# Attention with the weighted sum in full float32 on two halves of the array's columns

## The chip, the cores and the metric

One core of one Trainium2 chip runs the whole program. The metric is device time in microseconds (us), the median of three runs. A core has a matrix engine (TensorE, PE in the rows; its loads of the stationary operand are listed as PEld), VectorE (DVE), ScalarE (ACT), GpSimd (POOL) and the queues that issue DMAs (SP and ACT here). The engines run at the same time and wait for one another through semaphores; each works through its own list of instructions in order.

## The reference

The program chains three blocks. Attention is masked by a hash: a query sees only keys with the same six sign bits. Then comes a gated block with a mix over positions, and a residual block.

```python
mask = q_bucket[:, :, :, None] == k_bucket[:, :, None, :]
scores = scale * np.matmul(q, k.transpose(0, 1, 3, 2))
scores = np.where(mask, scores, -1000000000.0)
attn = np.exp(scores - np.max(scores, axis=-1, keepdims=True))
attn = attn / (np.sum(attn, axis=-1, keepdims=True) + 1e-09)
out = np.matmul(attn, v)                      # (2, 8, 768, 64)
# gated block, x is (2, 768, 512)
h = np.maximum(x @ w_in, 0.0)                 # 512 -> 1024, halves u and v
v_n = (v - mu) / np.sqrt(var + 1e-06)
v_s = np.einsum('ts,bsd->btd', w_spatial, v_n) + b_spatial[None, :, None]
x = (u * v_s) @ w_out                         # 512 -> 512
# residual block
ch = np.maximum(layernorm(x) * g_ln @ w_ch1, 0.0) @ w_ch2   # 512 -> 2048 -> 512
return x + ch
```

All matrices are float32, the weights `w_in`, `w_out`, `w_ch1` and `w_ch2` arrive as 64-bit floats. There are 2 batches, 8 heads, 768 positions and a head width of 64.

## The kernel before

**Tiles.** A tile is 128 queries of one head: 6 per head, 96 in all, in the list `order` (batch, head, group, tile). Two tiles make a group (`GRP = 2`), so there are 48 groups. `attn_step(i)` writes the work of step i: the transposes of tile i, the scores of tile i+2, the row maximum and the exponentials of tile i+1, and the weighted sum of the group that ended at tile i-1.

**Two kinds of product.** Where a float32 product is wanted exactly, the kernel mostly splits both operands into a high part of the type float32r and a rest, and adds the three products high-high, high-rest, rest-high (`mm3`). A product of plain float32 operands, as in `mismatch` (L245, output `pm`), is one call, and stands in the trace as two records.

**One tile.** `scores` (L303, `sc`) multiplies queries by 768 keys. `masked_max` (L314, DVE) takes the row maximum out of PSUM into `x`, `exps` (L327, ACT) the exponentials. `transposes` (L343, `pt`) turns the tile's six blocks of 128 x 128 around, three to a PSUM bank. ACT copies each bank out as float32r, `eh` (L352). For the first bank DVE takes the rest, `el` (`e_lo`, L360). For the second bank of every tile of batch 0, and of every other tile of batch 1 (`ES`), ACT copies to `es` (L347), and GpSimd makes `eh` (L77) and `el` (L86). `head_prep3` loads a head's values `vv` and GpSimd splits them as well (`vs`).

**Weighted sum.** `weighted` (L372, `po`) issues twelve matmuls for a group: six key tiles with `eh`, six with `el`. Each has the two parts of the values side by side as its 128 columns and 256 queries moving. The two halves of the result are then added: ACT copies the lower partitions' partner out as `ol` (L376), DVE adds (L378). `normalized` divides by the sums after every second head (`zr`, `zw`, `pz`, L383 to L393).

**Conversions.** The 64-bit weights of the gated block are converted in twelve pieces during attention, at the steps `CONV_AT`: ACT issues the load and takes the magnitude (L102), DVE makes five passes (L103 to L107), GpSimd adds (L111), ACT and GpSimd split (L80, L86). The result stays in SBUF for batch 0, in pieces of 1 MB of a ring of five (`WB`), and is written to DRAM, from where `reload` fetches it for batch 1.

**Stages.** From step 60 (`M0`) the gated block of batch 0 (`moe1(0)`) is woven into the steps of batch 1's attention: projections `pv`, mix `pg`, transposes `ptr`, output `py`. After the last step comes `moe1(1)`, with the first five pieces of the residual block, then the rest of that block (`up`, `pc`; `down`, `acc`) with 32 more conversions. The order on each engine is set by the tile scheduler, which lists the instructions by a timeline of its own; `issue_after` pins keep some of them behind others.

## Time and profile before

| | us |
|---|---|
| three runs: median (lowest, highest) | 748.74 (748.3, 752.26) |
| the profiled execution | 745.25 |
| its span | 743.5 |
| PE busy in it | 688.4 (93%) |
| DVE busy | 468.0 (63%) |
| ACT busy | 339.1 (46%) |
| POOL busy | 333.9 (45%) |

The busy shares are means over unlike stages, so the rows further down cut the span at four points: the first exponentials' maximum (13.4), the first projection of the gated block (186.2), the end of batch 0's gated block (356.5), and 480. A PE record lasts until its result is written, and the next one starts before that; the time that a run of matmuls takes is read from start to start.

### The profile page before, as it was taken

The numbers are of one execution on the slowest core, as the hardware profiler recorded it, in microseconds if no ns is written. First come the engines' busy times: TensorE is split into PE (matmuls) and PEld (weight loads), VectorE is DVE, ScalarE is ACT, GpSimd is POOL, SyncE is SP. The second block draws the span as 40 slices with busy tenths as digits, with TensorE's granted clock in tenths as the row PEclk, the third lists the DMA queues.
The fourth block names the chain that finished last, engine by engine and source line by source line (L and its number), as shares of the span: only waits on it lengthen the run. The fifth ranks groups of instructions, "written<-read, shape, count | busy, mean of one in ns | idle before, by whom it ended". The sixth has DMA issues, their size and how long they took to land.

```text
span 743.5 us, 10402 instructions
## 1 busy us (share of the span) xinstructions
PE 688.4 (93%) x3580; PEld 567.5 (76%) x3580; DVE 468.0 (63%) x873; ACT 339.1 (46%) x679; POOL 333.9 (45%) x358
## 2 busy tenths in 40 slices
PE   7899988899899998999889999799988999999996
PEld 6688867688788877888677887678766788888885
DVE  4677989889786964545399648776998712112112
ACT  3687867787566655545346332443323300100100
POOL 2788898998586672421035233235444400000000
PEclk9999999999999999999998999989999999999999
DMA  5645655657526336243703433343233101001001
GB/s 143 158 123 150 168 167 153 179 150 212 173 65 173 92 82 163 66 133 143 276 29 142 121 123 132 131 153 114 85 106 93 57 1 56 1 0 57 1 0 58
DMA packets 52519, 82.31 MB, mean 111 GB/s; under 512 B 7050, under 2 KB 36286, under 8 KB 50930
## 3 DMA queue, kind: packets, MB, share of 16 engines
q1 hardware_dynamic: 29714, 47.56, 22.8%
q10 hardware_dynamic: 22752, 34.08, 14.4%
q8 instruction: 29, 0.48, 0.3%
q14 instruction: 24, 0.20, 0.1%
HBM read 49.03 MB, written 12.58 MB: 83 GB/s over the span
## 4 chain that ended last, share of the span: by engine, by line
PE 49%; DVE 16%; DMA 11%; POOL 11%; issue 6%; ACT 5%; SPq 1%; ACTq 0%; DVEq 0%; POOLq 0%
PE acc L751 12%; PE pc L453 11%; PE pv L453 6%; DMA f_w<-in_w 5%; PE sc L303 4%; PE pg L453 4%; PE po L372 4%; PE pt L343 3%; POOL el L86 3%; PE py L453 2%; DMA wst_sp<-in_w_spT 2%; DVE f_w L105 2%; POOL f64c_w L111 2%; DVE f64c_w L107 2%; POOL eh L77 1%
## 5 line engine op out<-in xcount | busy, mean ns | idle before, releaser
L751 PE MATMUL acc<-w2t,ch 128*128 128x512 f32 x576 | 145.3, 397 | 6.9 <-DVE ch L742 6.1
L453 PE MATMUL pc<-xh,w1t 128*128 128x512 f32 x576 | 146.1, 400 | 3.4 <-DVE xh L735 3.2
L751 PEld LDWEIGHTS acc<-w2t,ch 128*128 128x128 f32 x576 | 107.4, 189 | 34.8 <-DVE ch L742 9.4
L453 PEld LDWEIGHTS pc<-xh,w1t 128*128 128x128 f32 x576 | 109.8, 191 | 30.2 <-ACT f64c_w L102 3.2
L742 DVE SCALAR_TENSOR_TENSOR ch<-pc,ch 128x512 fp32r<-128x512 f32 x48 | 32.9, 686 | 112.2 <-ACT ch L741 112.2
L327 ACT ACTIVATE x<-x,nb 128x768 f32<-128x768 f32 x96 | 89.5, 933 | 29.4 <-DVE x L314 29.3
L314 DVE TENSOR_SCALAR_CACHE_REDUCE x<-sc 128x768 f32<-128x768 f32 x96 | 89.6, 948 | 19.0 <-PE sc L303 11.3
L303 PE MATMUL sc<-ks,qs 128*128 128x512 f32 (+3 forms) x384 | 83.8, 353 | 8.0 <-issue 4.5
L343 PE MATMUL pt<-ident,x 128*128 128x128 f32 x576 | 84.1, 275 | 5.0 <-ACT es L347 2.8
L741 ACT ACTIVATE ch<-pc 128x512 fp32r<-128x512 f32 x48 | 28.4, 592 | 125.4 <-PE pc L453 124.7
L111 POOL TENSOR_TENSOR f64c_w<-f_w,f64c_w 128x512 f32<-128x512 f32 x32 | 44.7, 1400 | 89.6 <-DVE f64c_w L107 76.0
L343 PEld LDWEIGHTS pt<-ident,x 128*128 128x128 f32 x576 | 68.1, 141 | 15.6 <-ACT es L347 4.0
L86 POOL TENSOR_TENSOR el<-es,eh 128x384 fp32r<-128x384 f32 x72 | 78.3, 1089 | 3.0
L453 PE MATMUL pv<-w_in,act_x 128*128 128x512 f32 x288 | 75.6, 418 | 4.1 <-DMA w_in<-ws_in 3.5
L360 DVE TENSOR_TENSOR el<-pt,eh 128x384 fp32r<-128x384 f32 x120 | 64.0, 548 | 22.6 <-ACT eh L352 18.1
L453 PEld LDWEIGHTS pv<-w_in,act_x 128*128 128x128 f32 x288 | 56.6, 201 | 17.3 <-DMA w_in<-ws_in 4.0
L303 PEld LDWEIGHTS sc<-ks,qs 128*128 128x128 f32 (+1 forms) x384 | 57.3, 192 | 15.3 <-issue 5.6
L352 ACT ACTIVATE eh<-pt 128x384 fp32r<-128x384 f32 x120 | 56.1, 487 | 27.7 <-PE pt L343 26.3
L372 PE MATMUL po<-eh,vs 128*128 128x256 f32 x288 | 52.0, 304 | 7.1 <-POOL eh L77 4.9
L77 POOL TENSOR_SCALAR eh<-es 128x384 fp32r<-128x384 f32 x72 | 41.5, 579 | 36.9 <-ACT es L347 36.9
L372 PE MATMUL po<-el,vs 128*128 128x256 f32 x288 | 49.7, 290 | 1.2 <-DVE el L360 0.4
L372 PEld LDWEIGHTS po<-eh,vs 128*128 128x128 f32 x288 | 39.7, 190 | 13.2 <-POOL eh L77 7.3
(127 smaller groups left out, 981.7 us busy)
## 6 DMA issues: line engine op xcount, KB each, us to landing
f_w<-in_w ACTq DMA_DIRECT2D x32, 512.0 KB
ks<-k SPq DMA_DIRECT2D x48, 192.0 KB
qs<-q SPq DMA_DIRECT2D x144, 64.0 KB
wst_sp<-in_w_spT ACTq DMA_DIRECT2D x12, 384.0 KB
f_in<-in_w_in ACTq DMA_DIRECT2D x8, 512.0 KB
ws_in<-w_in ACTq DMA_DIRECT2D x4, 1024.0 KB
w_in<-ws_in SPq DMA_DIRECT2D x4, 1024.0 KB
vv<-in_v SPq DMA_DIRECT2D x16, 192.0 KB
```

Source lines behind the costliest of these rows:

```text
L77: nc.gpsimd.tensor_scalar(dst, src, 1.0, 0.0, op0=ALU.mult, op1=ALU.add)
L86: nc.gpsimd.tensor_tensor(dst, src, hi.bitcast(F32), op=ALU.subtract)
L111: nc.gpsimd.tensor_tensor(cf, tf, cf, op=ALU.add)
L303: nc.tensor.matmul(sc[:, csl], qs[:rows, i, qsl], ks[:rows, i, csl], start=(i == 0), stop=(i == 1))
L314: last["max"] = nc.vector.tensor_scalar(x, t["sc"], MASKED, FMAX, op0=ALU.min, op1=ALU.min, accum_out=nb,).ins
L327: last["exp"] = nc.scalar.activation(t["x"], t["x"], AF.Exp, bias=t["nb"], scale=-1.0, accum_out=z_sum[b][:, n, h : h + 1]).ins
L343: nc.tensor.transpose(pt[:, i, :], t["x"][:, kt * P : (kt + 1) * P], ident)
L352: nc.scalar.activation(eh, pt, AF.Copy)
L360: nc.vector.tensor_tensor(gr["el"][:, sl, qsl], t["pt"][c], gr["eh"][:, sl, qsl].bitcast(F32), op=ALU.subtract)
L372: nc.tensor.matmul(po[:, :GW], w, gr[e][:, kt, :], start=(n == 0), stop=(n == len(parts) - 1))
L453: mm = nc.tensor.matmul(ps, lh(i), rh(j), start=(n == 0), stop=(n == tot - 1)).ins
L751: last["mm"] = nc.tensor.matmul(accs[c][t], ch[:, i, t * P : (t + 1) * P], w2t[f][:, j, 0, :], start=(start and n == 0), stop=(stop and n ...
```

## The change

The exponentials are no longer split. A group's tile is one float32 tile `e`; ACT copies the first bank of each tile into it, DVE the second (plain copies out of PSUM, L340 and L342 in the new numbering). The values stay float32 as loaded. The weighted sum is six float32 matmuls with 64 columns each; the even key tiles write partitions 0 to 63 of the bank, the odd ones partitions 64 to 127, through the lower and the upper half of the array's columns. The two halves are added as before. It is issued one step later (`PO = 2`), the sums of a pair of heads another step, and the division two steps after that. `e` has three buffers.

The conversions start at step 5 instead of 20 and end at 57, and come in the order `w_out`, v half of `w_in`, u half. All three are kept in DRAM, in blocks of 2 MB. Two slots of 2 MB hold the v half, the u half, `w_out` and then the v and u halves and `w_out` of batch 1, each fetched when a slot is free. `w_out`, converted first, stays in the tile `vn` only until it is written out. The pieces of `w_spatial` are loaded from SP instead of ACT, have a tile for each part, and the mix uses the rests first.

```diff
-    CONV_AT = (20, 26, 32, 38, 43, 48, 52, 56, 62, 67, 72, 77)
+    CONV_AT = (5, 9, 14, 19, 24, 29, 34, 39, 44, 49, 53, 57)
-    AT = (-9, -8, -7, -4, 0)
-    ES = ((1,), (1, 0))
-    WB = 5
+    AT = (-10, -7, -6, -4, 0)
+    PO = 2
+    EB = 3
...
-            nc.scalar.dma_start(out=st, in_=src)
+            nc.sync.dma_start(out=st, in_=src)
...
-        vs = ap.tile([P, NKT, 2, D], F32R, tag="vs", name=f"vs_{nm}")
-        split_hi(vs[:, :, 0, :], vv)
-        split_lo(vs[:, :, 1, :], vv, vs[:, :, 0, :])
-        heads[b, h]["vs"] = vs
+        heads[b, h]["vv"] = vv
...
+            gr["e"] = ap.tile([P, NKT, GW], F32, tag="e", name=f"e_{b}_{h}_{g}", bufs=EB)
...
-            eh = gr["eh"][:, c * 3 : c * 3 + 3, qsl]
-            if c == 1 and ES[b][(g * GRP + j) % len(ES[b])]:
-                es = ap.tile([P, 3, P], F32, tag="es", name=f"es_{jm}", bufs=2)
-                nc.scalar.activation(es, pt, AF.Copy)
-                split_hi(eh, es)
-                split_lo(gr["el"][:, c * 3 : c * 3 + 3, qsl], es, eh)
+            e = gr["e"][:, c * 3 : c * 3 + 3, qsl]
+            if c == 0:
+                nc.scalar.activation(e, pt, AF.Copy)
             else:
-                nc.scalar.activation(eh, pt, AF.Copy)
+                nc.vector.tensor_copy(e, pt)
...
-        for n, (kt, e) in enumerate(parts):
-            w = vs[:, kt].rearrange("p a d -> p (a d)")
-            nc.tensor.matmul(po[:, :GW], w, gr[e][:, kt, :], start=(n == 0), stop=(n == len(parts) - 1))
+        for kt in range(NKT):
+            a = kt % 2 * D
+            nc.tensor.matmul(
+                po[a : a + D, :GW], heads[b, h]["vv"][:, kt], gr["e"][:, kt], start=(kt < 2), stop=(kt >= NKT - 2)
+            )
...
-        if 0 <= i - 1 < NT and order[i - 1][3] == GRP - 1:
-            weighted(*order[i - 1][:3])
+        if 0 <= i - PO < NT and order[i - PO][3] == GRP - 1:
+            weighted(*order[i - PO][:3])
+        for late, e in ((1, summed), (3, normalized)):
...
+        for key, src, at in (("out", w_out, 0), ("v", w_in, HF), ("u", w_in, 0)):
...
+    def moe_tile(key, b):
+        wp[key, b] = mp.tile([P, 2, KFT, HF], F32R, tag="w", name=f"w_{key}_{b}", bufs=2)
+        return wp[key, b]
...
+            if t == NQT - 1:
+                reload("out", b)
...
+        if b == 0:
+            reload("v", 1)
...
-    reload(w_in_pieces() + w_out_pieces(), 1)
+    reload("u", 1)
```

The matrix engine, around the weighted sum of group 1 of head 3 (`po_3_1`), batch 0, before. `sc` are scores, `pt` transposes; the last number counts equal instructions in a row.

```order
L303 MATMUL sc_4_0_0_1050<-ks_4_0_996,qs_4_0_991 128x512 x2
L343 MATMUL pt_3_2_0_0_1037<-ident,x_3_2_0_1025 128x128 x3
L343 MATMUL pt_3_2_0_1_1042<-ident,x_3_2_0_1025 128x128 x3
L372 MATMUL po_3_1_1060<-eh_3_1_950,vs_3_791 128x256 x6
L343 MATMUL pt_3_2_1_0_1081<-ident,x_3_2_1_1055 128x128 x3
L372 MATMUL po_3_1_1060<-el_3_1_951,vs_3_791 128x256 x3
L343 MATMUL pt_3_2_1_1_1086<-ident,x_3_2_1_1055 128x128 x3
L372 MATMUL po_3_1_1060<-el_3_1_951,vs_3_791 128x256 x3
```

The same place on the same engine after:

```order
L299 MATMUL sc_4_0_0_909<-ks_4_0_863,qs_4_0_858 128x512 x2
L337 MATMUL pt_3_2_0_0_899<-ident,x_3_2_0_882 128x128 x3
L337 MATMUL pt_3_2_0_1_904<-ident,x_3_2_0_882 128x128 x3
L337 MATMUL pt_3_2_1_0_928<-ident,x_3_2_1_914 128x128 x3
L337 MATMUL pt_3_2_1_1_933<-ident,x_3_2_1_914 128x128 x3
L351 MATMUL po_3_1_946<-e_3_1_838,vv_3_690 64x256 x6
```

Twelve matmuls in three runs, between transposes, have become six in one run behind all the transposes of the group that follows.

GpSimd in the steps of heads 3 and 4, batch 0, before (`eh`, `el` and `vs` are the split parts, `f64c` a conversion):

```order
L77 TENSOR_SCALAR eh_3_1_950<-es_3_1_0_961 128x3x128
L86 TENSOR_TENSOR el_3_1_951<-es_3_1_0_961,eh_3_1_950 128x3x128
L77 TENSOR_SCALAR eh_3_1_950<-es_3_1_1_1017 128x3x128
L86 TENSOR_TENSOR el_3_1_951<-es_3_1_1_1017,eh_3_1_950 128x3x128
L77 TENSOR_SCALAR eh_3_2_1035<-es_3_2_0_1046 128x3x128
L389 TENSOR_SCALAR zw_1_0_1184<-zr_1_1180 128x384
```

The same engine after, at the division of the same pair of heads (`zw_1`):

```order
L373 TENSOR_SCALAR zw_1_0_1109<-zr_1_1043 128x384
L373 TENSOR_SCALAR zw_1_1_1116<-zr_1_1043 128x384
L86 TENSOR_TENSOR w_out<-f64c_out_831,w_out 128x512
L111 TENSOR_TENSOR f64c_v_988<-f_v_956,f64c_v_988 128x512
L228 TENSOR_SCALAR k_0_3_1051<-k_0_3_1051 128x768
L86 TENSOR_TENSOR w_v_1086<-f64c_v_988,w_v_1086 128x512
```

No step of the exponentials is left on GpSimd; conversions, the splits of `k` and `q` and the divisors follow one another.

The matrix engine at the end of batch 0's gated block (`py_5`) and the start of batch 1's (`pv_0_1` is its first projection), after:

```order
L351 MATMUL po_7_2_3773<-e_7_2_3698,vv_7_3397 64x256 x6
L376 MATMUL pz_3_0_3788<-ident,zw_3_0_3786 128x128 x3
L376 MATMUL pz_3_1_3795<-ident,zw_3_1_3793 128x128 x3
L437 MATMUL py_5_3757<-w_out_2793,act_g_5_3754 128x512 x10
L437 MATMUL pv_0_1_3832<-w_v_3005,act_x_0_3824 128x512 x12
L437 MATMUL pv_1_1_3865<-w_v_3005,act_x_1_3828 128x512 x12
L437 MATMUL pv_0_0_3924<-w_u_3812,act_x_0_3824 128x512 x12
```

The third product of batch 1 is the first that needs `w_u`, whose slot `py_5` gives free; before, the first product read all four pieces of `w_in`.

## Rows read from the trace of the kernel before

**Rows 1.** Stages of the span: length, busy time (instructions) of each engine, clock, DMA.

```profile
core 0: us, PE busy (x) PEld busy (x) DVE busy (x) ACT busy (x) POOL busy (x), PEclk, DMA share, GB/s
...
13.40:186.20 172.80, 153.23 (x1038) 131.38 (x1039) 143.63 (x290) 132.54 (x293) 149.97 (x175) 1.00 0.60 161
186.20:356.50 170.30, 162.55 (x942) 138.21 (x941) 113.29 (x227) 99.76 (x209) 85.82 (x87) 0.98 0.42 121
356.50:480.00 123.50, 113.53 (x497) 91.09 (x496) 86.05 (x177) 47.80 (x82) 36.93 (x27) 0.96 0.40 133
```

**Rows 2.** One stretch of 20 us in the first stage, same columns.

```profile
150.00:170.00 20.00, 19.08 (x129) 16.30 (x128) 18.07 (x37) 16.31 (x38) 19.29 (x21) 1.00 0.55 158
```

**Rows 3.** GpSimd's costliest groups in the first stage: busy us, mean ns, idle before.

```profile
L86 POOL TENSOR_TENSOR el<-es,eh 128x384 fp32r<-128x384 f32 x54 | 58.8, 1091 | 1.7
L77 POOL TENSOR_SCALAR eh<-es 128x384 fp32r<-128x384 f32 x54 | 32.0, 595 | 12.5 <-ACT es L347 12.4
...
L86 POOL TENSOR_TENSOR vs<-vv,vs 128x384 fp32r<-128x384 f32 x10 | 10.4, 1042 | 0.1
```

**Rows 4.** Exponentials (L327, two records to a tile) in the first two stages.

```profile
13.40:186.20 172.80, 63.08 (x124) 1.00 0.60 161
186.20:356.50 170.30, 34.41 (x68) 0.98 0.42 121
```

**Rows 5.** The chain that ended last, second stage: start, us taken, what.

```profile
203.94 1.40 PE sc L303 x8
205.34 0.66 PE pt L343 x6
206.00 1.42 PE po L372 x12
207.42 2.58 PE pm L245 x8
210.00 2.77 PE pv L453 x12
...
298.97 4.13 PE pg L453 x18
...
305.57 0.55 PE pz L391 x3
...
311.62 0.44 PE ptr_g L440 x4
```

**Rows 6.** Matmul records of the weighted sum: ns min/median/max, first and last start.

```profile
L372 PE MATMUL po<-eh,vs x288: 274/281/577, 21.0 to 351.2; 128*128 128x256 f32 x144
```

**Rows 7.** VectorE in order of time: start, us, instruction (first stage).

```profile
66.77 0.95 DVE L314 TENSOR_SCALAR_CACHE_REDUCE x<-sc 128x768 f32<-128x768 f32 x1
67.64 0.09 DVE L314 DVE_READ_ACCUMULATOR x<-sc 128x1 f32 x1
67.64 0.56 DVE L360 TENSOR_TENSOR el<-pt,eh 128x384 fp32r<-128x384 f32 x1
...
173.27 0.54 DVE L360 TENSOR_TENSOR el<-pt,eh 128x384 fp32r<-128x384 f32 x1
173.73 0.41 DVE L104 TENSOR_SCALAR f64c_in<-f64c_in 128x512 uint32<-128x512 uint32 x1
```

**Rows 8.** VectorE's share of the conversions (five passes each), first stage.

```profile
13.40:186.20 172.80, 27.27 (x35) 1.00 0.60 161
```

**Rows 9.** The same of the residual block's conversions, third stage.

```profile
356.50:480.00 123.50, 31.77 (x60) 0.96 0.40 133
```

**Rows 10.** ScalarE's copies of the transposed tile, first stage.

```profile
L352 ACT ACTIVATE eh<-pt 128x384 fp32r<-128x384 f32 x67 | 32.0, 487 | 13.6 <-PE pt L343 12.9
```

**Rows 11.** VectorE's rests of the exponentials, first stage.

```profile
L360 DVE TENSOR_TENSOR el<-pt,eh 128x384 fp32r<-128x384 f32 x66 | 35.5, 548 | 5.7 <-ACT eh L352 4.9 <-POOL el L86 0.4
```

**Rows 12.** The chain at the end of batch 0's gated block.

```profile
355.34 7.24 DMA w_in<-ws_in
```

**Rows 13.** The matrix engine in order of time behind it.

```profile
362.62 24.05 PE L453 MATMUL pv<-w_in,act_x 128*128 128x512 f32 x99 [3.54 <-DMA w_in<-ws_in]
```

**Rows 14.** GB/s that the DMAs moved, in 40 equal slices of the span.

```profile
GB/s 143 158 123 150 168 167 153 179 150 212 173 65 173 92 82 163 66 133 143 276 29 142 121 123 132 131 153 114 85 106 93 57 1 56 1 0 57 1 0 58
```

More of the change, by code (lines that the diff above doesn't have):

```diff
@@ L511, in reload, with converted, stage, words @@
-    def reload(pieces, b):
-        for key, nk, n, _ in pieces:
-            wp[key, b] = mp.tile([P, 2, nk, n], F32R, tag="w", name=f"w_{key}_{b}", bufs=WB)
-            nc.sync.dma_start(out=wp[key, b].bitcast(F32), in_=w_split[key])
+    def converted(src, dst, nm, after=None):
+        d = {}
+        def stage():
+            d["st"] = stage_f64(src, nm)
+        def words():
+            d["tc"] = words_f64(d["st"], nm)
+        def join():
+            d["f"] = join_f64(*d["tc"])
+        def finish():
+            to = dst()
+            split_f64(to[:, 0], to[:, 1], d["f"])
+            if after:
+                after(to)
+        return stage, words, join, finish
@@ new lines, in kept, with conversions, dst, after @@
+    def kept(key, shape, to):
+        w_split[key] = dram.tile(shape, F32, tag=f"ws_{key}", name=f"ws_{key}")
+        nc.scalar.dma_start(out=w_split[key], in_=to.bitcast(F32))
+    def moe_tile(key, b):
+        wp[key, b] = mp.tile([P, 2, KFT, HF], F32R, tag="w", name=f"w_{key}_{b}", bufs=2)
+        return wp[key, b]
+    def conversions():
+        res = []
+        for key, src, at in (("out", w_out, 0), ("v", w_in, HF), ("u", w_in, 0)):
+            for k in range(KFT):
+                def dst(key=key, k=k):
+                    if k == 0:
+                        if key == "out":
+                            wp[key] = mp.tile([P, 2, NKT, HF], F32R, tag="vn", name="w_out", bufs=1)
+                        else:
+                            wp[key] = moe_tile(key, 0)
+                    return wp[key][:, :, k : k + 1]
+                def after(to, key=key):
+                    kept(key, [P, 2, KFT, HF], wp.pop(key)[:, :, :KFT])
+                src_k = src[:, k : k + 1, at : at + HF]
+                res.append(converted(src_k, dst, f"{key}_{k}", after if k == KFT - 1 else None))
+        return res
@@ L516, in moe1, with reload @@
+    def reload(key, b):
+        nc.sync.dma_start(out=moe_tile(key, b).bitcast(F32), in_=w_split[key])
     def moe1(b, ps_m, tag):
-        wi = [wp[f"in{k}", b] for k in range(KFT)]
         vn = mp.tile([P, 2, NKT, HF], F32R, tag="vn", name=f"vn_{b}", bufs=1)
@@ L607, in moe1 @@
                 pg = ps_m.tile([P, 512], F32, tag=tag, name=f"pg_{nm}")
-                mm3(
-                    pg,
-                    [(lambda i, k=k: w[:, i, k, :], lambda j, k=k: vn[:, j, k, :]) for k in range(NKT)],
-                )
+                order3 = [(k, 1, 0) for k in range(NKT)] + [(k, 0, j) for k in range(NKT) for j in range(2)]
+                for n, (k, i, j) in enumerate(order3):
+                    nc.tensor.matmul(pg, w[i][:, k], vn[:, j, k, :], start=(n == 0), stop=(n == len(order3) - 1))
                 gt = mp.tile([P, HF], F32, tag="tmp", name=f"gt_{nm}", bufs=TB)
@@ L618, in moe1 @@
                 ga = gas.pop(t - 1)
-                wo = [wp[f"out{k}", b] for k in range(KFT // 2)]
+                wo = wp["out", b]
                 py = ps_m.tile([P, 512], F32, tag=tag, name=f"py_{b}_{t - 1}")
@@ L652, in attn_moe_kernel @@
     head_prep3(0, 0)
[L653 removed]
+    convs = conversions()
     conv_steps = {}
@@ L659, in attn_moe_kernel @@
     n0 = 0
-    for i in range(-1 - QA, NT + 3):
+    for i in range(-1 - QA, NT + PO + 3):
         attn_step(i)
```

77 lines of the change are left out of this document (16 added, 61 removed).

## The prediction

> **What bounds the kernel now.** The stages come first [rows 1]. In the first, 172.8 us long, no engine is idle much: PE 153.2, GpSimd 150.0, VectorE 143.6. A shorter stretch tells them apart: from 150 to 170 GpSimd is busy 19.29 of 20 us, 96% [rows 2]. Its list shows with what: rests and high parts of the exponentials, 58.8 and 32.0 us, and 10.4 us for rests of the values [rows 3]. So the stage goes at GpSimd's pace once the conversions run, and one tile takes 172.8 / 62 = 2.79 us [rows 4].
>
> PE's busy time counts the tail of each record, so I add up its work from start to start [rows 5]. First stage: 31 pairs of tiles' scores at 1.40, 62 sets of six transposes at 0.66, 30 weighted sums at 1.42, five mask products of 2.58 (eight records), eight divisors of 0.55: 43.4 + 40.9 + 42.6 + 12.9 + 4.4 = 144.2 us of 172.8. PE has 28 us to spare there.
>
> Second stage, 34 tiles [rows 4] and the gated block of batch 0: 17 x 1.40, 34 x 0.66, 18 x 1.42, 2 x 2.58, seven divisors of 0.55, eighteen products of twelve matmuls at 2.77, six of eighteen at 4.13, six sets of transposes at 0.44 = 23.8 + 22.4 + 25.6 + 5.2 + 3.9 + 49.9 + 24.8 + 2.6 = 158.2 of 170.3 us. Here PE is the bound, and 12.1 us are waits. Behind it PE waits once for the reload of `w_in` [rows 12, 13].
>
> **The change part by part.**
>
> *GpSimd* loses all steps of the exponentials and of the values: over 101 of its 150 us in the first stage [rows 3]. It keeps the splits of q and k, the divisors and the conversions, of which there are now eleven or twelve instead of seven. At about 60 us it bounds nothing.
>
> *VectorE* had 143.6 us [rows 1]. Conversions were 27.3 of it [rows 8]. The rests of the exponentials are 66 instructions [rows 11]; each holds up the next one for 0.46 us (173.27 to 173.73) [rows 7], less than its record of 0.548, together 30.4. What stays is 86.0. New are 62 copies out of PSUM. The trace has no such copy on this engine; the nearest row is the rest it replaces, of the same shape with one operand more, 0.46 us, and on the other side ScalarE's copy of this shape, 0.487 [rows 10]. I take 0.46, 28.5 us; at 0.40 it would be 24.8. Eleven conversions lie in the stage, since all start earlier. One took 27.27 / 7 = 3.90 us beside the full GpSimd [rows 8], and 31.77 / 12 = 2.65 in the third stage, where GpSimd is busy 36.9 of 123.5 us [rows 1, 9]. The emptied GpSimd is nearer to the second: I take 3.0, 33 us, with 29 and 43 as ends. Sum 147.5 us, ends 140 and 159. VectorE does not become lighter; it changes the passes that it does.
>
> *ScalarE* loses the second copy of nearly every tile, some 60 at 0.487 [rows 10], 29 of its 132.5 us. It was not the bound; this is worth nothing by itself.
>
> *PE, the weighted sum.* The price of a float32 product is in the mask product: eight records of 384 columns in 2.58 us [rows 5], 0.32 each, so 0.215 for 256 columns. A group has six products, twelve records. If the halves of the columns do not work at the same time, that is 12 x 0.215 = 2.58 us instead of 1.42. If they do, the two records of one key tile still follow each other, as they use the same columns, and the second of one goes together with the first of the next: seven steps, 1.50 us. With perfect pairs it would be 1.29. The trace of before has no matmul on part of the columns, so 1.29 and 2.58 are the ends. I take 1.50, as the change puts neighbours on different halves. That adds 2.4 us to PE's first stage (146.6) and 1.5 to its second.
>
> The Trainium skill (TensorE: Matmul & The Clock Gate, Part 3) says that matmuls on different column groups run concurrently, and gives 2.38 times for three groups; no run here shows it. By that rule the price is the lower one, without it 2.58.
>
> *First stage.* PE with 146.6 and VectorE with 147.5 us are now level. The busiest engine was busy 87% of this stage over its whole length and 96% in the dense stretch [rows 1, 2]. I take 92%: 147.5 / 0.92 = 160.3, **12.5 us less**. At 87% it is 169.5 (3 less), at 97% 152 (21 less). The first steps, which had no conversions, get five of them.
>
> *Second stage.* PE's work is 159.7. Of the 12.1 us of waits, those for GpSimd's parts and for the last conversions can go; I keep 8: 167.7, **2.6 less**, with ends 9 less and 2 more.
>
> *The reload.* The u half of batch 1 is 2 MB and its fetch waits for the last product with `w_out`. Two products, 5.5 us, run before it is needed. In the slice where two fetches of 1 MB ran together the DMAs moved 276 GB/s [rows 14], so 7.6 us; one fetch alone took 7.24 for 1 MB, with others beside it [rows 12], so at worst 14.5. PE would wait 2.1 to 9 us where it now waits 3.54 [rows 13]. I take no change, with ends 1.4 less and 5.5 more. The loads of `w_spatial` and the extra fetch of `w_out` go through SP, where the q and k rows of the next heads stand behind them; the next heads are prepared several steps ahead, so this costs nothing unless a fetch sits there waiting for its slot. The later sums and divisions are covered by the next groups' steps. The last group's sum and division stand ahead of the last `py`, as before.
>
> Together 15 us off the profiled execution: 745.25 - 15 = 730. It lay 3.5 us under the median, so on the median's scale **734**. The ends add up to 29 less and 5 more, 720 to 754, and are not all met at once: 722 to 746 is this case's own range.
>
> **The rivals.**
>
> *The halves do not overlap.* Then a group costs 2.58 us. In the first stage PE needs 144.2 + 30 x 1.16 = 179, and at 96% that is 186, 13 more than now; VectorE would wait for it. In the second, the bound is PE anyway: 18 x 1.16 = 20.9 more, less the 4 us of waits, 17. Together 30 more: 775 + 3.5 = 779. Without the recovered waits and with a denser first stage it could be 770. This is also the case in which the change does not do what it says. For it speaks that no row shows two matmuls at once; against it that the two halves have separate columns and separate partitions of PSUM. The deciding price: PE overtakes VectorE's 147.5 at 1.53 us to a group. At 2.0 the first stage is (144.2 + 30 x 0.58) / 0.96 = 168, only 4.6 less than now, and the second 18 x 0.58 - 4 = 6.4 more. So from about 2.0 us to a group the kernel is slower than before.
>
> *Going over to half columns and back costs PE a drain each time.* A record of 256 columns lasts 281 ns [rows 6], yet twelve follow each other in 1.42 us, 0.118 apart: a tail of 0.16 that is normally hidden. Two changes to a group show it twice, 0.33 us. First stage: PE 146.6 + 9.9 = 156.5, at 95% 164.7, 8 less than now. Second: 159.7 + 5.9 + 8 = 173.6, 3.3 more. Together 5 less: 744.
>
> The Trainium skill (TensorEngine Tiling (Array Packing), Key Properties) states that a change of the tiling mode drains TensorE, a rule against this change; the tail above is what it would cost here, and no run of before shows it.
>
> **How the numbers follow.** Forecast 0.56, no overlap 0.27, drain 0.17. A measurement of this kernel tells 0.5%, 3.7 us, from no change. The forecast is faster in nearly all its range (0.51 of 0.56, 0.03 same, 0.02 slower), the drain case sits near the line (0.09 faster, 0.06 same, 0.02 slower), no overlap is slower (0.27). Together faster 0.60, same 0.09, slower 0.31. The range has to reach into the case without overlap, as more than 0.2 lies there: up to 777 leaves about 0.13 out above; 721 leaves 0.05 out below.
>
> **What would show it.** The weighted sum's six float32 matmuls: twelve records in about 1.5 us from the first start to the next instruction's, with starts of lower and upper half 0.2 us or less apart; 2.6 us shows no overlap. A gap of 0.16 us ahead of the first and behind the last shows the drain. VectorE's copy near 0.46 us to the next start, a conversion's five passes near 3.0. The first stage near 160 us with PE and VectorE both over 90%, GpSimd near 60 us. The second near 168. A wait of PE for `w_u` near 3.5 us behind two products of batch 1. The forecast falls if a group costs over 2 us, or if the conversions, now close together, stay at 3.9 us and hold the maxima back behind them in VectorE's list.

## The result and the profile after

The changed kernel takes **736.62 us** (median of four runs, 734.81 to 737.87) against 748.52 us of the kernel before on the same chip (four runs, 748.25 to 752.26): a ratio of **0.983, interval 0.980 to 0.986**, or 12 us less. The forecast was 734. Its reasons did much worse than its number, as the rest of this document shows.

The profiled execution took 737.13 us, its span is 734.9. Against the profiled execution of before that is 8.1 us less, where the sum had said 15; the medians are 12 apart because before's profiled run lay under its median and this one lies on it.

The first two stages of the kernel after, cut at the same events as [rows 1]: first maximum, first projection of the gated block, end of batch 0's gated block. Columns: stretch, length, busy time (instructions) of each engine, granted clock (PEclk, 1.00 is the full speed), DMA share, GB/s.

```profile
core 0: us, PE busy (x) PEld busy (x) DVE busy (x) ACT busy (x) POOL busy (x), PEclk, DMA share, GB/s
16.18:183.70 167.52, 151.84 (x1017) 111.48 (x1018) 139.96 (x299) 112.66 (x236) 56.04 (x54) 0.97 0.65 179
183.70:350.00 166.30, 162.42 (x950) 124.08 (x949) 88.22 (x190) 83.32 (x168) 37.75 (x33) 0.99 0.41 120
```

GpSimd fell from 150 to 56 us in the first stage, and that stage became only 5.3 us shorter. Even this is too kind a reading: the first projection now stands at another step, so the cut moved. A cut that cannot move is a tile. These are the 96 row maxima in the kernel after and in the one before (duration min/median/max in ns, first and last start in us):

```profile
L310 DVE TENSOR_SCALAR_CACHE_REDUCE x<-sc x96: 935/950/959, 16.2 to 332.8; 128x768 f32<-128x768 f32 x96
```

```profile
L314 DVE TENSOR_SCALAR_CACHE_REDUCE x<-sc x96: 883/950/958, 13.4 to 340.3; 128x768 f32<-128x768 f32 x96
```

With the maximum of tile 60 (from VectorE in order of time) and the last `py` the span falls into five parts. Each column is one profiled execution. The two right columns are experiments told further down; the profiled execution of weighted_late is its fastest, 3.4 us under its median:

| us | before | after | weighted_only | weighted_late |
|---|---|---|---|---|
| start to the first maximum | 13.4 | 16.2 | 17.5 | 12.9 |
| tile 0 to tile 60 | 166.7 | 164.8 | 172.5 | 159.0 |
| tile 60 to tile 95 | 160.2 | 151.8 | 164.9 | 152.9 |
| tile 95 to the last `py` | 137.1 | 135.9 | 129.3 | 131.8 |
| the rest | 266.1 | 266.2 | 266.8 | 265.0 |
| span | 743.5 | 734.9 | 751.0 | 721.6 |

So the start lost 2.8 us, sixty tiles gained 1.9, and the gain of 8.4 lies in the tiles that run beside the gated block.

**The start.** SP's queue and the matrix engine at the beginning, in order of time (start, us, instruction, idle before):

```profile
3.99 0.43 SPq L191 DMA_DIRECT2D wst_sp<-in_w_spT  x1
5.51 0.54 SPq L269 DMA_DIRECT2D ks<-k  x1
```

```profile
13.27 2.90 PE L299 MATMUL sc<-ks,qs 128*128 128x512 f32 x8 [3.09 <-DMA qs<-q]
18.15 2.90 PE L299 MATMUL sc<-ks,qs 128*128 128x512 f32 x8 [1.98 <-issue]
20.85 2.30 PE L337 MATMUL pt<-ident,x 128*128 128x128 f32 x12
```

The granted clock is the figure ahead of the last two of this row:

```profile
14.00:16.00 2.00, 2.00 (x8) 1.35 (x6) 0.00 (x0) 0.00 (x0) 0.00 (x0) 0.50 0.32 72
```

A load of `w_spatial`, wanted only in the gated block, now stands ahead of the first keys and queries. Its pin names an instruction of ScalarE; the load is on SP, and is issued at 3.99 all the same, where a pin on an instruction of SP holds it until 245 (start_sp). PE idles 3.09 us, in which the granted clock falls to 0.5, the lower of its two levels (1.2 GHz). It stays there from 12.3 to 22.5, and eight score matmuls take 2.70 us (18.15 to 20.85) that take 1.40 to 1.50 elsewhere.

**The weighted sum** of a group, from the transposes ahead of it to the instruction behind:

```profile
62.36 0.82 PE L337 MATMUL pt<-ident,x 128*128 128x128 f32 x6
63.10 1.52 PE L351 MATMUL po<-e,vv 128*64 128x256 f32 x12
64.55 0.91 PE L245 MATMUL pm<-k,sides 128*128 128x384 f32 x2
```

From start to start the twelve records take 1.45 us. The six transposes ahead take 0.74, where they take 0.57 ahead of scores: 0.17 more. So a group costs 1.62; full_cols, below, shows that the 0.17 do not all lie ahead.

**VectorE** in the first stage: its copies, and the five passes of the first four conversions (busy us, mean ns, idle before).

```profile
L342 DVE COPY e<-pt 128x384 f32<-128x384 f32 x60 | 32.9, 548 | 3.6 <-PE pt L337 3.2
...
L105 DVE SCALAR_TENSOR_TENSOR f_out<-f_out,f64c_out 128x512 uint32<-128x512 uint32 x4 | 3.4, 855 | 0.0
...
L107 DVE SCALAR_TENSOR_TENSOR f64c_out<-f_out,f64c_out 128x512 f32<-128x512 uint32 x4 | 2.7, 677 | 0.0
...
L103 DVE TENSOR_SCALAR f64c_out<-f64c_out 128x512 f32<-128x512 f32 x4 | 1.7, 427 | 1.8 <-ACT f64c_out L102 1.6
L104 DVE TENSOR_SCALAR f64c_out<-f64c_out 128x512 uint32<-128x512 uint32 x4 | 1.7, 422 | 0.1
L106 DVE TENSOR_SCALAR f64c_out<-f_out 128x512 uint32<-128x512 uint32 x4 | 1.7, 413 | 0.0
```

The five means add up to 2.79 us, against 3.90 before [rows 8].

**The reload** behind batch 0, PE at the first product with `w_u`:

```profile
361.77 2.99 PE L437 MATMUL pv<-w_u,act_x 128*128 128x512 f32 x12 [2.79 <-DMA w_u<-ws_u]
```

### The profile page after: what moved, and what is told of

Its sections match the earlier page's. It is cut to its first block, busy times and chain, and to the rows that moved or that the text cites. A ratio compares the mean times of both kernels' runs of the same rounds, so it can differ in the third digit from the quotient of the medians.

```text
span 734.9 us, 9990 instructions
## 1 busy us (share of the span) xinstructions
PE 686.0 (93%) x3580; PEld 533.1 (73%) x3580; DVE 438.7 (60%) x849; ACT 303.6 (41%) x583; POOL 190.9 (26%) x182
## 3 DMA queue, kind: packets, MB, share of 16 engines
q10 hardware_dynamic: 13040, 29.36, 12.3%
## 4 chain that ended last, share of the span: by engine, by line
PE 60%; DVE 15%; DMA 11%; ACT 4%; issue 4%; POOL 3%; SPq 1%; DVEq 0%; ACTq 0%; POOLq 0%
PE acc L747 12%; PE pc L437 11%; PE sc L299 7%; DMA f_w<-in_w 7%; PE pv L437 7%; PE pt L337 6%; PE pg L607 6%; PE po L351 6%; PE py L437 3%; POOL f64c_w L111 2%; DVE f_w L105 2%; DVE x L310 2%; DMA qs<-q 2%; DMA f_v<-in_w_in 1%; DVE f64c_w L107 1%
## 5 line engine op out<-in xcount | busy, mean ns | idle before, releaser
L337 PE MATMUL pt<-ident,x 128*128 128x128 f32 x576 | 79.8, 278 | 9.8 <-ACT x L323 9.3
L351 PE MATMUL po<-e,vv 128*64 128x256 f32 x576 | 74.1, 393 | 0.4 <-DVE m L246 0.4
L340 ACT ACTIVATE e<-pt 128x384 f32<-128x384 f32 x96 | 46.5, 488 | 45.4 <-PE pt L337 44.5
L342 DVE COPY e<-pt 128x384 f32<-128x384 f32 x96 | 52.7, 549 | 20.7 <-PE pt L337 20.2
L351 PEld LDWEIGHTS po<-e,vv 128*64 128x64 f32 x576 | 37.5, 138 | 24.4 <-issue 7.3
L102 ACT ACTIVATE f64c_w<-f_w 128x512 f32<-128x512 f32 x32 | 21.4, 669 | 63.0 <-DMA f_w<-in_w 59.6
L607 PE MATMUL pg<-vn,w_sp 128*128 128x512 f32 x180 | 44.1, 397 | 0.0
L437 PE MATMUL pv<-w_u,act_x 128*128 128x512 f32 x144 | 37.8, 398 | 4.7 <-DMA w_u<-ws_u 2.8
L607 PEld LDWEIGHTS pg<-vn,w_sp 128*128 128x128 f32 x180 | 33.3, 188 | 7.6
L437 PE MATMUL py<-w_out,act_g 128*128 128x512 f32 x144 | 35.8, 396 | 2.1 <-ACT act_g L426 2.1
```

Of the source, the lines that this page charges most:

```text
L337: nc.tensor.transpose(pt[:, i, :], t["x"][:, kt * P : (kt + 1) * P], ident)
L340: nc.scalar.activation(e, pt, AF.Copy)
L342: nc.vector.tensor_copy(e, pt)
L351: nc.tensor.matmul(po[a : a + D, :GW], heads[b, h]["vv"][:, kt], gr["e"][:, kt], start=(kt < 2), stop=(kt >= NKT - 2))
L437: mm = nc.tensor.matmul(ps, lh(i), rh(j), start=(n == 0), stop=(n == tot - 1)).ins
L607: nc.tensor.matmul(pg, w[i][:, k], vn[:, j, k, :], start=(n == 0), stop=(n == len(order3) - 1))
```

## The experiments

All ratios are to the kernel before on the same chip in the same session, with 95% intervals. The kernel after has 0.983 [0.980, 0.986]. The sessions are on different chips, so two experiments are best compared by their ratios. The edits are cut to the lines that matter.

### Do the halves overlap, and what does the change of mode cost?

**no_overlap**: all key tiles on the lower half.

```diff
-            a = kt % 2 * D
-                po[a : a + D, :GW], heads[b, h]["vv"][:, kt], gr["e"][:, kt], start=(kt < 2), stop=(kt >= NKT - 2)
+                po[0:D, :GW], heads[b, h]["vv"][:, kt], gr["e"][:, kt], start=(kt == 0), stop=(kt == NKT - 1)
-        nc.scalar.activation(ol, po[D:P, :GW], AF.Copy)
+        nc.scalar.activation(ol, po[0:D, :GW], AF.Copy, scale=0.0)
```

> The changed kernel with all six key tiles on the lower half of the columns (the other half's addend is ScalarE's copy times zero). Theory: two halves work at the same time; on one half the twelve records follow each other at 0.215 us, 2.58 and more to a group instead of 1.45. PE has 48 x 1.13 = 54 us more, of which waits in the first stage take up some 10: 780 to 790. Rival: a record of 64 columns is quicker by itself, 0.12 us, and the halves have nothing to do with it: 737, and a group stays at 1.45.

Measured: 785.18 us, ratio 1.050 [1.045, 1.054]. One group:

```profile
62.49 0.82 PE L337 MATMUL pt<-ident,x 128*128 128x128 f32 x6
63.24 2.80 PE L350 MATMUL po<-e,vv 128*64 128x256 f32 x12
65.97 0.85 PE L299 MATMUL sc<-ks,qs 128*128 128x512 f32 x3
```

2.73 us, so a record of 64 columns is not quicker by itself, and the second half halves the time. 2.73 is 12 x 0.215 + 0.15, and 1.45 is 6 x 0.215 + 0.16: after the change the records run in six full pairs, with about 0.15 on top. The starts of the single records in the trace say the same: the two of a pair stand 0.007 us apart, the pairs 0.216. The Trainium skill (TensorE: Matmul & The Clock Gate, Part 3) says that column groups work concurrently; the trace agrees, at twice the rate for two halves.

**full_cols**: 128 columns for each matmul (the values of a key tile and the next, behind the last a block of zeros; the upper half's result is multiplied by zero).

```diff
-            a = kt % 2 * D
+            w = heads[b, h]["vv"][:, kt : kt + 2].rearrange("p a d -> p (a d)")
-                po[a : a + D, :GW], heads[b, h]["vv"][:, kt], gr["e"][:, kt], start=(kt < 2), stop=(kt >= NKT - 2)
+            nc.tensor.matmul(po[:, :GW], w, gr["e"][:, kt], start=(kt == 0), stop=(kt == NKT - 1))
```

> The changed kernel with 128 columns to a weighted sum's matmul (the values of a key tile and of the next; only the lower 64 rows are used). Theory: twelve records of 0.215, 2.58 to a group, and no gap ahead of the weighted sum, since the array stays whole: six transposes ahead of it take 0.57 us to its start, as they do ahead of scores, not 0.75. So a little under the kernel with all key tiles on one half, by up to 48 x 0.33 = 16 us: 768 to 785. Rival on the gap: it comes from going from float32r to float32 matmuls; then 0.75 stays and the two kernels are level. Rival on the price: 128 columns cost the same as 64 on one half only if the record's price hangs on the 256 moving columns; if it hangs on the columns of the array, this one takes 1.45 x 2 or more.

Measured: 778.68 us, 1.041 [1.038, 1.045].

```profile
115.42 0.82 PE L338 MATMUL pt<-ident,x 128*128 128x128 f32 x6
116.08 2.76 PE L352 MATMUL po<-e,vv 128*128 128x256 f32 x12
118.48 1.77 PE L300 MATMUL sc<-ks,qs 128*128 128x512 f32 x8
120.09 1.47 PE L338 MATMUL pt<-ident,x 128*128 128x128 f32 x12
121.40 2.76 PE L352 MATMUL po<-e,vv 128*128 128x256 f32 x12
123.99 0.82 PE L338 MATMUL pt<-ident,x 128*128 128x128 f32 x6
124.56 0.71 PE L300 MATMUL sc<-ks,qs 128*128 128x512 f32 x2
```

The price is that of one half: 64 or 128 stationary columns cost the same at 256 moving ones. Where transposes follow, the twelve records take 2.59 us (12 x 0.215 = 2.58), with no tail. Where scores follow it is 2.40, but nothing is won by that: the first score record starts 0.03 us behind the start of the last record, and the second one 0.42 later instead of 0.23. For the same reason six transposes take 0.57 ahead of scores and 0.65 (6 x 0.109) ahead of this product; ahead of half columns they take 0.75. So 0.09 us are lost ahead of half columns. Behind them, taken to the second record of what follows, half columns (no_overlap) lie 0.20 us behind full columns where transposes follow and 0.25 where scores or a mask product follow. Together that is 0.29 to 0.34 to a group, all of it with the half columns. So the expected theory on the gap stands in substance, and the rival (float32r to float32) falls, although the 0.57 of the theory is not the figure to compare with. The Trainium skill (TensorEngine Tiling (Array Packing), Key Properties) states that a change of tiling mode drains TensorE; the trace agrees, with 0.09 us ahead and 0.20 to 0.25 behind.

**halves_apart**: the order of the key tiles.

```diff
-        for kt in range(NKT):
+        for kt in (0, 2, 4, 1, 3, 5):
```

> The changed kernel with the key tiles in the order 0, 2, 4 (lower half), then 1, 3, 5 (upper half). Theory: a record runs beside the one behind it in PE's list, so only neighbours on different halves overlap; with the halves apart one pair of records is left, eleven steps of 0.215 and a drain, 2.5 us to a group, and the kernel takes 775 to 790. Rival: the halves have queues of their own, and the order among six matmuls does not matter: 1.45 to a group, 736 to 738.

Measured: 753.12 us, 1.012 [1.009, 1.015]; a group takes 1.93 us:

```profile
58.84 2.00 PE L351 MATMUL po<-e,vv 128*64 128x256 f32 x12
60.77 0.87 PE L337 MATMUL pt<-ident,x 128*128 128x128 f32 x6
```

Both expectations fell. The records that are under way in two stretches of 0.4 us of it (the number behind the x):

```profile
59.20:59.60 0.40, 0.40 (x6) 1.00 0.39 87
59.60:60.00 0.40, 0.40 (x7) 1.00 0.52 115
```

One half alone, with a record every 0.216 us, has at most four in such a stretch. So the upper half starts before the lower is through: 1.93 - 0.15 - 6 x 0.215 = 0.49 us behind it, not 1.08. The starts of the twelve records agree: they form two series of six, one from 58.84, the other from 59.33, where the lower half has begun only its third record. PE takes up later work for the other half, but the order still costs 0.48 us to a group.

**two_groups**: the weighted sums of two groups in one run, one bank, `e` with four buffers.

```diff
-    EB = 3
+    EB = 4
-        if 0 <= i - PO < NT and order[i - PO][3] == GRP - 1:
-            weighted(*order[i - PO][:3])
+        if 0 <= i - PO < NT and (i - PO) % (2 * GRP) == 2 * GRP - 1:
+            weighted(order[i - PO - GRP][:3], order[i - PO][:3])
```

> The changed kernel with the weighted sums of two groups issued in one run (24 records, one bank of PSUM, e with four buffers, the first group's two steps later). Theory: a group costs six perfect pairs of 0.215, 1.29 us, and each going over to half columns and back costs 0.16 to 0.17 more; one run of two groups then takes 2.75 from its start to the next instruction's instead of 2 x 1.45, and one gap of 0.17 ahead of it is saved, together 0.33 for two groups. PE has 24 x 0.33 = 8 us less: 729 to 735. Rival: a group costs seven steps of 0.21 and no drain: two groups take 2.9, and the time stays at 736 to 738.

Measured: 773.18 us, 1.038 [1.034, 1.042]: far slower, although the price is as expected. PE in order of time, at two places:

```profile
55.60 1.81 PE L299 MATMUL sc<-ks,qs 128*128 128x512 f32 x8 [2.44 <-issue]
...
71.22 2.81 PE L351 MATMUL po<-e,vv 128*64 128x256 f32 x24
73.96 1.22 PE L299 MATMUL sc<-ks,qs 128*128 128x512 f32 x6
```

24 records take 2.74 = 12 x 0.215 + 0.16, so the seven steps fall for good. But PE now stands idle ahead of the scores, 33.2 us in 15 places of the first stage. VectorE at the first place:

```profile
54.54 0.95 DVE L310 TENSOR_SCALAR_CACHE_REDUCE x<-sc 128x768 f32<-128x768 f32 x1
```

The scores of a group have one buffer for both tiles (`ps_s`, one), and the next group's start at 55.60, right behind the end of this second maximum (55.49). The profile names no releaser; the time of the maximum does. The weighted sum is the work that PE has meanwhile; where every second group has none, it waits. That is read from this place, and no run with a second buffer tests it. The granted clock is lower, too: 0.96 in the mean of the span, in the kernel after 0.98. **start_two** (this and start_act's edit together) gave 772.91, 1.037 [1.035, 1.040], the same.

> Both at once: the pieces of w_spatial issued by ScalarE, and the weighted sums of two groups in one run. If the start and the drains are what the first stage lost, the two gains add up: 722 to 728. If VectorE bounds the first stage once PE has less, only the start's gain and that of the second stage (9 x 0.33 = 3 us) show: 727 to 732.

### Was GpSimd the bound?

**pool_load**: GpSimd splits the second half of each tile again, and nobody reads it.

```diff
+            if c == 1:
+                eh = ap.tile([P, 3, P], F32R, tag="dh", name=f"dh_{jm}", bufs=1)
+                el = ap.tile([P, 3, P], F32R, tag="dl", name=f"dl_{jm}", bufs=1)
+                split_hi(eh, e)
+                split_lo(el, e, eh)
```

> The changed kernel with GpSimd's split of the exponentials put back as idle work (two instructions for the second half of each tile, 0.60 and 1.09 us; nobody reads what they write). GpSimd's first stage goes from 56 to about 160 us. Theory: GpSimd set the pace of the first stage before. Then that stage goes from 167.5 to 172 or more, and VectorE's five passes of a conversion from 2.8 to near 3.9 us, since they run beside a full GpSimd: 742 to 750. Rival: GpSimd was only as busy as the others, and PE and VectorE hold the stage at 167 us; then 737 to 739.

Measured: 748.18 us, 1.002 [0.999, 1.005]: with a full GpSimd the whole gain is gone. Tile 0 to 60 takes 171.2 us (164.8 without), 60 to 95 154.8 (151.8). VectorE's passes beside it:

```profile
L107 DVE SCALAR_TENSOR_TENSOR f64c_out<-f_out,f64c_out 128x512 f32<-128x512 uint32 x4 | 4.7, 1171 | 0.0
L105 DVE SCALAR_TENSOR_TENSOR f_out<-f_out,f64c_out 128x512 uint32<-128x512 uint32 x4 | 3.7, 932 | 0.0
L103 DVE TENSOR_SCALAR f64c_out<-f64c_out 128x512 f32<-128x512 f32 x4 | 2.9, 737 | 1.4 <-ACT f64c_out L102 1.3
L104 DVE TENSOR_SCALAR f64c_out<-f64c_out 128x512 uint32<-128x512 uint32 x4 | 2.4, 602 | 0.1
L106 DVE TENSOR_SCALAR f64c_out<-f_out 128x512 uint32<-128x512 uint32 x4 | 2.0, 509 | 0.0
```

3.95 us a conversion instead of 2.79 in these four, 3.65 in the four of the v half: as expected. GpSimd is busy 144 of the 171.2 us, VectorE 144.5 instead of 137.3. The idle work also reads `e`, but ScalarE waited for that only once, 0.7 us. So GpSimd's load does cost, 12 us by the medians and 14 by the ratios. That it alone set the pace does not follow: taking it away brought the sixty tiles 1.9 in the kernel after, and 7.7 in weighted_late, which leaves the conversions at their old steps.

### What holds the first stage now?

**copies_half**: the second copy of every other tile on ScalarE.

```diff
-            if c == 0:
+            if c == 0 or (g * GRP + j) % 2:
```

> The changed kernel with the second copy of every other tile on ScalarE instead of VectorE. VectorE's first stage goes from 140 to about 126 us, ScalarE's from 113 to about 128. Theory: VectorE is what the first stage waits for where conversions lie (its busy share is 93 to 100% there, and PE waits 9.3 us for exponentials that wait for maxima): 3 to 7 us shorter, 730 to 734. Rival: PE, with 1.62 us to a group and its drains, is the bound of the stage, and the time stays at 736 to 738.

Measured: 741.32 us, 0.993 [0.989, 0.996]: slower than the kernel after. VectorE is busy 123.9 us instead of 137.3 between tiles 0 and 60, and that takes 170.0 instead of 164.8. PE's waits there that the kernel after does not have:

```profile
PE sc L299 <- DMA ks<-k: 4.6, 1, 4.6
PE po L351 <- ACT e L340: 3.3, 4, 1.7
```

The wait for keys comes last, ahead of tile 60, and the granted clock is 0.5 behind it (179.1 to 185.9); more than half of the 5.2 us lies there. But already ahead of it, at tile 58, this kernel is 160.4 us behind its first maximum and the kernel after 158.4. So with less work VectorE let the stage go no faster. As the work went to ScalarE, which PE then waits for, the run does not show what VectorE's work is worth by itself.

**conv_two**: two buffers for a conversion, its load three steps ahead.

```diff
-    CB0 = 1
+    CB0 = 2
-    CONV_D = (-1, 0, 3, 3)
+    CONV_D = (-3, 0, 3, 3)
```

> The changed kernel with two buffers for a conversion and its load three steps ahead instead of one. ScalarE stands 9.5 us in the first stage at the head of its list for loads of conversions (f_v 4.9, f_u 3.5, f_out 1.1), with exponentials behind, and PE waits 9.3 us for exponentials. Theory: these waits set the first stage; they go, and it gets 3 to 6 us shorter: 730 to 734. Rival: PE's own work and the one buffer of the scores, which PE and VectorE use in turn, set it: 735 to 738.

Measured: 748.76 us (741.64 to 752.13), 1.003 [1.000, 1.006]. ScalarE's waits for loads of `f_v` and `f_u` are gone from its list, and the kernel is slower: first maximum at 16.8, tile 60 at 187.6. The theory fell, and more than the rival said was lost. Half of the loss comes at one wait of PE for keys (4.6 us), new as in copies_half, with a granted clock of 0.5 behind it (183.9 to 190.7); where the rest came from stays open.

**start_act** and **start_sp**: the loads of `w_spatial` from ScalarE as before, or from SP but pinned behind the load of a head's values.

```diff
-            nc.sync.dma_start(out=st, in_=src)
+            nc.scalar.dma_start(out=st, in_=src)
```

> The changed kernel with the pieces of w_spatial issued by ScalarE again, as before the change. Theory: the changed kernel loses its time at the start, since the first piece (384 KB) stands in SP's list ahead of the first rows of q and k; they land at 13.0, PE idles 3.1 us ahead of the first scores, and the scores then take 2.90 us a pair instead of 1.5 until about 22. Then the first maximum comes near 13.4 instead of 16.2, the first scores take 1.5, and the kernel is 5 to 7 us shorter, 730 to 732. Rival: PE and VectorE have enough to catch up on later, since the loads of heads and the conversions set the pace of the first stage: 0 to 3 us shorter, 734 to 737.

```diff
-            if "late" in last:
-                pins.enter_context(tc.issue_after(last["late"]))
+            pins.enter_context(tc.issue_after(last["sp"]))
...
-        nc.sync.dma_start(out=vv, in_=v[b, :, h])
+        last["sp"] = nc.sync.dma_start(out=vv, in_=v[b, :, h]).ins
```

> The changed kernel with the pieces of w_spatial on SP as there, but held behind the last load of a head's values, so that the first two are not issued at the start. When ScalarE issued all pieces, the first maximum came 3.5 us sooner and tile 12's only 1.2, and the rest of the loss lay in batch 1's gated block (last product with w_out at 478.0 instead of 468.7), where ScalarE's own list held projections up. Theory: the start's gain is mostly given back by tile 12, and nothing is lost later: 734 to 736. Rival: with the loads at their places the start's 3.5 us and the half clock's 3 to 4 stay: 729 to 732.

Measured: start_act 743.75 us, 0.995 [0.993, 0.997]; start_sp 735.51, 0.985 [0.983, 0.987]. Both have the first maximum at 12.6 to 12.7, 3.5 us sooner, and tile 60 at 181.8 and 181.0, where the kernel after has 181.0: the gain at the start is real and is given back within the stage. start_act then loses 9 us in batch 1's gated block (last `py` at 478.0 instead of 468.7), where PE waits for projections that ScalarE's list holds up, and stands at a granted clock of 0.5 from 370.5 to 380.8:

```profile
PE pv L437 <- ACT xT L582: 9.7, 2, 8.4
```

So in this kernel the loads' place at the start costs little in the end, and their move to SP is worth about 9 us later.

### The weighted sum alone, and the delay

**weighted_only**: the kernel before with the new weighted sum, the copies and the unsplit values that it needs, and nothing else.

```diff
-        for n, (kt, e) in enumerate(parts):
-            w = vs[:, kt].rearrange("p a d -> p (a d)")
-            nc.tensor.matmul(po[:, :GW], w, gr[e][:, kt, :], start=(n == 0), stop=(n == len(parts) - 1))
+        for kt in range(NKT):
+            a = kt % 2 * D
+            nc.tensor.matmul(
+                po[a : a + D, :GW], heads[b, h]["vv"][:, kt], gr["e"][:, kt], start=(kt < 2), stop=(kt >= NKT - 2)
+            )
...
-                nc.scalar.activation(es, pt, AF.Copy)
-                split_hi(eh, es)
-                split_lo(gr["el"][:, c * 3 : c * 3 + 3, qsl], es, eh)
...
+            if c == 0:
+                nc.scalar.activation(e, pt, AF.Copy)
...
-                nc.scalar.activation(eh, pt, AF.Copy)
+                nc.vector.tensor_copy(e, pt)
```

> The kernel before with the weighted sum's part of the change alone: e and the values not split, six float32 matmuls on two halves of the columns, second copy on VectorE; one step behind as before, conversions at steps 20 to 77, the ring of five pieces and ScalarE's loads of w_spatial as before. Tile 60's maximum came at 180.1 us before and 181.0 after, the last one at 340.3 and 332.8: the gain lies in the second stage. If unsplitting makes it (VectorE and GpSimd give PE no more waits there): 737 to 741, with the 160 us from tile 60 to 95 down to 153 or less. If the conversions, which now end ahead of that stage, make it: 745 to 749, and the 160 us stay above 157.

Measured: 753.52 us, 1.009 [1.006, 1.012]: slower than before. One of its groups:

```profile
103.23 1.08 PE L350 MATMUL po<-e,vv 128*64 128x256 f32 x6
104.23 0.91 PE L245 MATMUL pm<-k,sides 128*128 128x384 f32 x2
...
105.72 1.08 PE L350 MATMUL po<-e,vv 128*64 128x256 f32 x6
106.73 0.59 PE L245 MATMUL pm<-k,sides 128*128 128x384 f32 x1
```

One step behind, the second half of `e` is not ready, and the scheduler puts other work between: three key tiles (lower, upper, lower) are four steps and a tail, 4 x 0.215 + 0.15 = 1.01 us. Twice that, and 0.17 for each run, make 2.36 for a group instead of 1.62. The table shows a second loss: the first maximum comes at 17.5 instead of 13.4, since PE waits 4.2 us for the first queries; the start has the code of before, and why they came later was not told apart.

**weighted_late**: the same, two steps behind, with a third buffer of `e` (the division also comes one step later).

```diff
-            gr["e"] = ap.tile([P, NKT, GW], F32, tag="e", name=f"e_{b}_{h}_{g}")
+            gr["e"] = ap.tile([P, NKT, GW], F32, tag="e", name=f"e_{b}_{h}_{g}", bufs=3)
-        if 0 <= i - 1 < NT and order[i - 1][3] == GRP - 1:
-            weighted(*order[i - 1][:3])
+        if 0 <= i - 2 < NT and order[i - 2][3] == GRP - 1:
+            weighted(*order[i - 2][:3])
```

> The kernel of weighted_only with the weighted sum two steps behind instead of one (e with three buffers, the division one step behind it). In weighted_only 18 of the 48 groups stand in two runs of six records, 1.01 us each and 0.17 ahead of each, 2.36 together instead of 1.62, 13 us of PE in all; two steps behind, all 48 stand in one run. Theory: these second runs are why the part alone was slower, and the delay is what makes the half columns pay: 738 to 743. Rival: the part alone is slow for another reason (tile 0 to 60 took 172 us with the conversions of steps 20 to 62 as before, and the second stage keeps five conversions): 747 to 753.

Measured: **726.83 us** (723.42 to 729.92), 0.973 [0.969, 0.977]: faster than both kernels, the interval lies below that of the kernel after. Its group, and its two parts of tiles with the columns of the first table:

```profile
64.45 1.51 PE L350 MATMUL po<-e,vv 128*64 128x256 f32 x12
65.90 0.87 PE L337 MATMUL pt<-ident,x 128*128 128x128 f32 x6
```

```profile
12.90:171.90 159.00, 146.64 (x1002) 108.19 (x1004) 128.97 (x274) 105.91 (x224) 46.55 (x45) 0.99 0.61 165
171.90:324.80 152.90, 149.35 (x886) 115.19 (x888) 95.40 (x203) 82.92 (x168) 50.57 (x42) 1.00 0.47 137
```

Every group stands in one run. The step of delay, with the third buffer, is worth 27 us here, twice what the second runs cost by their price (18 x 0.74 = 13); 4.6 us of the rest is weighted_only's later start. Part of it is the granted clock: up to the last tile weighted_only stands at 0.5 for 27 us (from 12.5, 60.3, 224.1 and 336.7), weighted_late for 3.4 (from 16.3). What else is in it was not told apart, and the expected 738 to 743 was too high.

So the weighted sum with its delay gives 2.7%, and the other parts of the change (conversions from step 5, their order, the ring of 2 MB, the loads on SP, other steps for the preparation of heads) take a point of it back: 736.6 against 726.8. By the table, 13 us apart, they cost 3.3 us at the start, 5.8 in the first sixty tiles, 4.1 behind the last tile and 1.2 in the rest, and give 1.1 between. The first item is the load of `w_spatial`. For the second the traces have a reason that no run isolates: the kernel after begins eleven conversions there and not seven, and VectorE is busy 137 us and not 129. With the start put right (start_sp) 3.7 us are lost against weighted_late between tiles 4 and 12, where the first conversions meet the preparation of the second pair of heads:

```profile
38.20 0.87 PE L336 MATMUL pt<-ident,x 128*128 128x128 f32 x6 [2.21 <-ACT x L322]
38.83 2.46 PE L298 MATMUL sc<-ks,qs 128*128 128x512 f32 x8
```

From 29.93 to 36.14 VectorE works through the five passes of a conversion and steps of that preparation, with a maximum behind them in its list. PE waits 2.21 us for the exponentials of that maximum, and then the granted clock is 0.5 from 39.4 to 42.8, so that the eight scores take 2.26 us. The kernel after loses 4.5 us against weighted_late between tiles 40 and 44 in the same way: a pass waits 3.65 us for a late load of `f_v` with two maxima behind it, the next maximum stands behind passes and preparation until 136.59, PE waits 2.11 us for exponentials, and the clock is 0.5 from 138.6 to 142.0.

## Why the prediction was right, and where its steps were not

**Overlap of the halves: right.** It was the question on which the sign hung, and no_overlap shows the other side: 785 us, predicted 779.

**The price of a group: wrong mechanism, size near.** Taken were seven steps, 1.50 us, and no drain. It is six full pairs and a drain on both sides, 1.29 + 0.33 = 1.62. The drain rival had the 0.33 right, by luck in part, as it took the tail of a record for both sides; it had put them on top of seven steps. Forty-eight times 0.12 is 6 us that the sum lacks.

**The first stage, 12.5 us less: failed.** Measured were 5.3 by the cuts of [rows 1], 1.9 by tiles, and 2.8 lost ahead. The step "so the stage goes at GpSimd's pace" [rows 2] read a busy share as a bound: an engine at 96% in one stretch, with PE and VectorE over 90% there, was one of three. (The 87% of the same paragraph are GpSimd's 150.0; PE's busy time was 89%.) What GpSimd gave free was real: pool_load loses it again, and weighted_late takes 7.7 us off the sixty tiles. That the earlier conversions, the dearer group and the lower clock took most of it back is read from the traces and no run isolates it. The clock had no term in the sum: 9.7 us of this stage lie at 0.5, none before. The 92% were taken for VectorE, which was busy 84% (140.0 of 167.5); PE had 91%. The sign that the prediction named for its fall, conversions that hold maxima back in VectorE's list, is in the traces (tiles 40 to 44), though with conversions of 2.8 us and not of 3.9.

**VectorE: right in its terms.** A copy holds up the next instruction for about 0.47 us (0.46 taken), a conversion takes 2.79 (3.0), the stage has 140.0 (147.5, with 140 as the lower end). That it would be level with PE and share the bound is not borne out: with less work on it (copies_half) the stage went no faster.

**The delays: failed.** "The later sums and divisions are covered" is true, but the later weighted sum itself was given no price. It is the part without which the half columns do not pay: 753.5 us without it, 726.8 with it.

**The loads on SP: failed.** "This costs nothing unless a fetch sits there waiting" looked at the heads in mid-run. The first load went to the front of the list, as the order of SP's queue shows, and cost 2.8 us there. In batch 1 the move gains.

**Second stage: sign right, size low.** 4.0 us less by the cuts, 8.4 by tiles, against 2.6 with 9 as the far end. The trace of before shows what went. Its two longest waits from tile 60 to 95 are one for GpSimd's divisors (1.94 us) and one ahead of scores (2.53, at 293.2), and behind each the granted clock is 0.5 for 3.4 us:

```profile
193.54 0.55 PE L391 MATMUL pz<-ident,zw 128*128 128x128 f32 x3 [1.94 <-POOL zw L389]
193.84 4.58 PE L453 MATMUL pv<-w_in,act_x 128*128 128x512 f32 x12
198.26 0.82 PE L343 MATMUL pt<-ident,x 128*128 128x128 f32 x6
```

The twelve matmuls take 4.42 us there, against 2.77 [rows 5]. So some 3 of the 12.1 us that the prediction counts as waits were the lower clock. In the kernel after both waits are gone, the clock is 1.00 throughout, and PE waits 2.7 us in all.

**The reload: right.** PE waits 2.79 us, predicted near 3.5, and the kernel loses nothing by it.

Summed up: the predicted 15 us stood against 8.1 in the profiled executions, and the forecast came within 3 us of the median because the run of before that was profiled lay 3.5 us low. That is luck, and so is part of the 8.1: the start and the first sixty tiles together lost 0.9 us where 12.5 were to be gained, and the tiles behind gained 5.8 more than was said.

## What to carry to other kernels

A matmul whose output has 64 rows can run two at a time on the halves of the columns in float32 too, but going over to half columns and back has to be paid at each run (here 0.33 us): put all such matmuls of a unit in one run, late enough that nothing has to come between, and leave other work for the matrix engine beside the vector engine's turn. Take the time of a stage from the index of a tile, not from an instruction that the change moves. When a load changes its queue, look whether what held it back still does. And a wait of the matrix engine can cost more than its length: look at the granted clock behind it.

## What the runs showed of the hardware

- Two float32 matmuls on the two halves of the columns run in full pairs: 1.45 us for twelve records, 2.73 on one half, 2.59 on all columns.
- Against all columns, a run of half columns costs 0.09 us ahead and 0.20 to 0.25 up to the second record of what follows. 0.15 of it stands ahead of the next instruction's start, whether the run has 6, 12 or 24 records (1.01, 1.45, 2.74 us).
- A float32r score starts 0.03 us behind the start of a last float32 record on all columns, but its second record then comes 0.42 later instead of 0.23.
- With the halves one after the other, the second starts 0.49 us behind the first and not behind its last record.
- In an idle of 3.09 us at the start the granted clock fell to 0.5 and stayed there for 10 us, in which eight scores took 2.70 us instead of 1.40 to 1.50. Idles of 1.94 to 2.53 us later were followed by 3.4 us at 0.5 (before, after, start_sp), one of 1.98 us at the start of the kernel before was not.
- VectorE's five passes over 128 x 512 words take 2.79 us where GpSimd is busy a third of the time (55 of 165 us), and 3.95 where it is busy 84%.
